# Attention on one core: the order of the maxima's products in a step, and where their results are turned and sent

## The chip, the core and the metric

One core of a Trainium2 chip: TensorE (PE, with its weight loads PEld), VectorE (DVE), ScalarE (ACT), GpSimd (POOL) and the DMA queue of SyncE (SP), each with its own queue of instructions and tied together by semaphores. The metric is the device time of one execution in microseconds, the median of the runs.

## The reference

A transformer block in float32: layer norm, attention with 32 heads of 20 columns over 2048 tokens, residual, layer norm, SwiGLU with 1728 hidden columns, residual.

```python
def _A_ref(x, wqkv, wo):            # B=1, S=2048, D=640, H=32, Dh=20
    qkv = (x @ wqkv).reshape(B, S, 3, H, Dh).transpose(2, 0, 3, 1, 4)
    q, k, v = qkv[0], qkv[1], qkv[2]
    scores = jnp.einsum("bhqd,bhkd->bhqk", q, k) * (Dh ** -0.5)
    p = _softmax(scores, axis=-1)
    o = jnp.einsum("bhqk,bhkd->bhqd", p, v)
    return o.transpose(0, 2, 1, 3).reshape(B, S, D) @ wo
def _B_ref(x, w_gate, w_up, w_down):
    return (_silu(x @ w_gate) * (x @ w_up)) @ w_down
h = x + _A_ref(_layernorm(x), A_wqkv, A_wo)
out = h + _B_ref(_layernorm(h), B_w_gate, B_w_up, B_w_down)
```

## The kernel before

The kernel has three stages: norm and projections of q, k and v; attention; output projection and feed-forward part. The change is in the attention.

Attention is cut into 32 **units**: a group `g` of four heads (8 groups) and a chunk `c` of 512 queries (4 chunks), `u = 4 g + c`. A unit has 16 **steps**, one for each tile `kt` of 128 keys. A step makes the four heads' scores (128 keys x 512 queries, L1328, functions `scores`), takes their exponential on ScalarE into `probs` (L1334), and weighs the values with the `probs` of two steps before (`weigh`, L1338, four heads at once in four column tiles of 32), summing into the bank `acc`. Heads lie in pairs in the two halves of the 128 rows: heads with `b = 0` use rows 0 to 63 of TensorE, those with `b = 1` rows 64 to 127.

The softmax subtracts each query's maximum. It must be known before a unit starts, since minus the maximum stands in extra rows of the unit's queries (`q_stk`) and is added by the score's own product. So in the steps of earlier units, **maxima** are worked out ahead: a product of 128 queries with 512 keys into one of three banks `ps_max` (L272), then a reduction on VectorE. A step makes three such banks. Two are whole ones for one head (`max_one`, reduced at L292). The third is split: the first half (256 keys, head `b = 0`) is written early in the step and the second half (256 keys, head `b = 1`) later, into the same bank, and one reduction gives both maxima (`max_half`, `max_halves`, reduced at L307). Ahead of the second half `next_half` puts a marker into TensorE's queue (L1411) that waits until the first half is written, so that the two row halves never write the bank at the same time.

The order of a step is written out by hand as a string, `ORDER`, which one loop reads letter by letter:

- `W` weighs, and runs what is due: functions put in `later` for this step, one step of the preparation of the feed-forward weights (`preparing`), and so on;
- `h` and `H`: first and second half of the split maximum; `m` and `M`: a whole one with `b = 0` and with `b = 1`;
- `S` and `s`: scores of a head with `b = 1` and with `b = 0`.

Banks of `ps_max` go round in threes, so a step's `h` takes the bank of the last step's `h`, `m` that of `m`, `M` that of `M`. The banks of the scores go round in fours.

When a unit's maxima are complete (`full`), `max_all` joins them (`neg`, L315). Then there are two ways. For units with `v % 4 == 3` and unit 1, `max_finish` turns them on TensorE (L347), ScalarE and VectorE split them into two parts (`m`), and four DMAs (L354) put them into the queries. For the others, `max_parts` splits on GpSimd, `max_turn` turns on VectorE (L331) and stores to memory, and `max_load` brings the rows back (L342).

In the second step of a unit the last weighing of the unit before is done. `row_sums` copies its `acc` to `o` on ScalarE (L1348) and sends the row sums to `r` (L1351). At later steps of that unit `reciprocals` (VectorE, L1359), `spread` (`rb`, L1367), `store_o` with a product on GpSimd (L1373) and its stores (L1376) follow. At fixed steps the loop also loads queries three units ahead (L176), and keys and values of the next group (L176, L193). All these DMAs share SP's queue, which issues in order: one that must wait holds back those behind it.

## Time and profile before

| | us |
|---|---|
| runs: median (lowest to highest of 3) | 2011.97 (2009.52 to 2014.36) |
| profiled execution, its own time | 2012.87 |
| its span | 2010.4 |
| TensorE busy, matmuls | 1985.1 (99%) |
| VectorE busy | 1599.5 (80%) |
| ScalarE busy | 1440.1 (72%) |
| GpSimd busy | 789.4 (39%) |

Busy time is the time in which at least one instruction of the engine ran. Instructions of one engine overlap, so the time from one start to the next can be shorter than the duration that the profile shows. In rows of groups the columns are line, engine, operation, output and inputs with their shapes and the count, then busy time and mean ns of one, then the engine's idle time before them and what ended it. In rows of a timeline they are start, duration, engine, line, operation, tiles, count, and in brackets the idle time before and what ended it.

### The profile page before, as it was taken

How to read it: one execution, taken by the hardware profiler on the slowest of the kernel's cores; microseconds unless marked ns; L12 is line 12 of the kernel's file. 1: busy time of each engine (PE TensorE's matmuls, PEld its weight loads, DVE VectorE, ACT ScalarE, POOL GpSimd, SP SyncE). 2: the span in 40 equal slices, each digit the busy share in tenths (PEclk: the TensorE clock that was granted, in tenths of full speed). 3: DMA queues.
4: the chain of work that ended last, by engine and by line, in shares of the span. 5: the costliest groups of instructions: out<-in, count | busy, mean ns of one | idle time of the engine just before them, and what ended most of it. 6: DMA issues, size and time to landing. Idle time of an engine off the chain costs nothing. (4 is left out here: it accounts for less than half of the span.)

```text
span 2010.4 us, 41923 instructions
## 1 busy us (share of the span) xinstructions
PE 1985.1 (99%) x14794; PEld 1268.7 (63%) x14794; DVE 1599.5 (80%) x2831; ACT 1440.1 (72%) x2827; POOL 789.4 (39%) x1182
## 2 busy tenths in 40 slices
PE   8999999999999999999999999999999999999998
PEld 6999995444444444444444444455598888888887
DVE  5687778899999899998999999975477666676667
ACT  4678778999999999999999999987633222212221
POOL 7464424343453443443400011011155544844465
PEclk9999999999999999999999999999999999999999
DMA  7887563443634544435412132222268655974642
GB/s 244 255 258 257 183 206 78 128 140 105 193 103 141 152 135 138 157 127 175 150 60 68 40 86 58 79 63 62 62 215 278 228 168 174 359 248 160 203 146 93
DMA packets 199350, 310.48 MB, mean 154 GB/s; under 512 B 53744, under 2 KB 87856, under 8 KB 198120
## 3 DMA queue, kind: packets, MB, share of 16 engines
q1 hardware_dynamic: 192552, 284.21, 44.0%
q0 software_dynamic: 6496, 23.60, 4.0%
q8 instruction: 120, 1.97, 0.4%
q14 instruction: 86, 0.70, 0.1%
q10 hardware_dynamic: 96, 0.00, 0.0%
HBM read 208.11 MB, written 99.19 MB: 153 GB/s over the span
## 5 line engine op out<-in xcount | busy, mean ns | idle before, releaser
L1334 ACT ACTIVATE probs<-ps_one 128x512 f32<-128x512 f32 x2048 | 1056.1, 612 | 46.7 <-PE ps_one L1328 37.2
L292 DVE TENSOR_REDUCE mx<-ps_max 128x1 f32<-128x512 f32 x980 | 671.8, 686 | 90.6 <-PE ps_max L272 88.0
L272 PEld LDWEIGHTS ps_max<-k_stk,q_stk 60*128 60x128 f32 x1964 | 294.2, 185 | 462.8 <-DVE mx L307 393.5
L1328 PE MATMUL ps_one<-q_stk,k_stk 62*128 62x512 f32 x2048 | 570.4, 427 | 2.7 <-DMA q_stk<-m 1.8
L272 PE MATMUL ps_max<-k_stk,q_stk 60*128 60x256 f32 (+1 forms) x1964 | 565.5, 376 | 2.5 <-DVE mx L292 1.2
L1338 PE MATMUL acc<-probs,v_stk 128*32 128x512 f32 x4096 | 546.1, 605 | 0.1
L307 DVE TENSOR_REDUCE mx<-ps_max 128x2 f32<-128x512 f32 x492 | 335.8, 683 | 0.4 <-PE ps_max L272 0.4
L1328 PEld LDWEIGHTS ps_one<-q_stk,k_stk 62*128 62x128 f32 x2048 | 304.9, 184 | 15.0 <-ACT probs L1334 11.3
L1750 DVE TENSOR_TENSOR tmp<-ps_a,tmp 128x512 f32<-128x512 f32 x208 | 141.3, 690 | 122.2 <-PE ps_a L1535 96.6
L262 DVE TENSOR_REDUCE mx<-ps_max 128x2 f32<-128x512 f32 x288 | 180.8, 685 | 63.7 <-PE ps_max L240 60.2
L252 ACT ACTIVATE ps_max<-ps_max 128x512 f32<-128x512 f32 x288 | 151.6, 583 | 42.9 <-PE ps_max L240 40.3
L1629 PE MATMUL ps_b<-halves,yp 128*128 128x320 f32 x1032 | 179.0, 308 | 1.5 <-DMA halves<-j_d 1.3
L1629 PEld LDWEIGHTS ps_b<-halves,yp 128*128 128x128 f32 x1032 | 165.2, 188 | 17.5 <-POOL yp L90 1.5
L1535 PE MATMUL ps_a<-t,units 128*128 128x512 f32 x624 | 162.5, 396 | 0.0
L1338 PEld LDWEIGHTS acc<-probs,v_stk 128*32 128x32 f32 x4096 | 80.7, 108 | 128.1 <-issue 119.9
L90 POOL TENSOR_TENSOR yp<-y,yp 128x256 fp32r<-128x256 f32 x96 | 60.2, 628 | 189.7 <-ACT yp L89 189.7
L1535 PE MATMUL ps_a<-z,units 128*128 128x512 f32 x516 | 133.8, 394 | 0.0
L1535 PEld LDWEIGHTS ps_a<-t,units 128*128 128x128 f32 x624 | 112.6, 188 | 18.5
L1373 POOL TENSOR_TENSOR o<-o,rb 128x512 f32<-128x512 f32 x31 | 39.8, 1284 | 194.2 <-DMA rb<-r_d 60.6
L1634 DVE TENSOR_TENSOR h<-ps_b,h 128x320 f32<-128x320 f32 x248 | 110.1, 482 | 6.8 <-PE ps_b L1629 5.4
L671 PE MATMUL ps_one<-z_hi,w_lo 64*128 64x512 f32 x380 | 113.4, 392 | 0.0
L671 PE MATMUL ps_one<-z_lo,w_hi 64*128 64x512 f32 x380 | 112.1, 392 | 0.0
(228 smaller groups left out, 2746.5 us busy)
## 6 DMA issues: line engine op xcount, KB each, us to landing
units<-w_d SPq DMA_DIRECT2D x186, 256.0 KB
w_d<-stage SPq DMA_DIRECT2D x106, 256.0 KB
halves<-j_d SPq DMA_DIRECT2D x70, 320.0 KB
j_d<-stage SPq DMA_DIRECT2D x42, 320.0 KB
k_stk<-k_d SPq DMA_DIRECT2D x64, 160.0 KB
q_stk<-q_d SPq DMA_DIRECT2D x64, 160.0 KB
raw<-k_d SPq DMA_DIRECT2D x62, 160.0 KB
raw<-q_d SPq DMA_DIRECT2D x54, 160.0 KB
```

Of the source, the lines that this page charges most:

```text
L252: nc.scalar.activation(ps, ps, AF.Relu)
L262: nc.vector.tensor_reduce(mx[:, b, :, t, kc], ps.rearrange("p (j n) -> p j n", j=2), axis=AX.X, op=ALU.max,)
L272: nc.tensor.matmul(ps, queries[u][rows, pair, t * P : (t + 1) * P], keys[u // NC][rows, pair, k0:k1], start=True, stop=True, skip_group_ch ...
L292: nc.vector.tensor_reduce(mx[:, b, pair, t, kc : kc + 1], ps, axis=AX.X, op=ALU.max)
L307: nc.vector.tensor_reduce(max_slots(u)[:, :, pair, t, slot], ps.rearrange("p (j n) -> p j n", j=2), axis=AX.X, op=ALU.max,)
L671: nc.tensor.matmul(ps, a[rows], b[rows], start=(i == n == 0), stop=(i == 1 and n == last), skip_group_check=True,)
L1328: nc.tensor.matmul(ps, keys[u // NC][rows, p, kt * P : (kt + 1) * P], queries[u][rows, p, :], start=True, stop=True,)
L1334: nc.scalar.activation(probs[p][:, b, :], ps, AF.Exp, scale=scale)
L1338: nc.tensor.matmul(acc[32 * j : 32 * j + 32, :], values[u // NC][:, kt, j * VW : j * VW + 32], probs[j // 2][:, j % 2, :], start=(kt == 0) ...
L1535: nc.tensor.matmul(ps.rearrange("p (t n) -> p t n", t=TPC), w[k][:, i], z[k][:, :, j], start=(first and m == 0), stop=(last and m == len(n ...
L1629: nc.tensor.matmul(ps, a, b, start=(n == 0), stop=(n == len(pairs) - 1))
L1750: add = lambda out, ps, x: nc.vector.tensor_tensor(out=out, in0=ps, in1=x, op=ALU.add)
```

## The change

```diff
-ORDER, LAST_ORDER = "WhSmsSHMs", "sSsSW"
+ORDER, LAST_ORDER = "WhSmsSMsH", "sSsSW"
...
         max_product(ps, u, t, pair, b, kc * CH, (kc + 1) * CH)
-        nc.vector.tensor_reduce(mx[:, b, pair, t, kc : kc + 1], ps, axis=AX.X, op=ALU.max)
+        return lambda: nc.vector.tensor_reduce(
+            mx[:, b, pair, t, kc : kc + 1], ps, axis=AX.X, op=ALU.max
+        )
...
         o = pc.tile([P, CH], F32, name="o", bufs=2)
-        nc.scalar.activation(o, acc, AF.Copy)
+        nc.vector.tensor_copy(o, acc)
...
             a = whole.pop(0)
-            max_one(*a)
-            counted(a[0], 1)
+            reduce = max_one(*a)
+
+            def reduced():
+                reduce()
+                counted(a[0], 1)
+
+            if b:
+                behind_half.append(reduced)
+            else:
+                reduced()
...
                     next_half(int(op == "H"))
+                    while behind_half and op == "H":
+                        behind_half.pop(0)()
...
-                    if preparing and u and kt not in (3, 4):
+                    if preparing and u and kt not in (3, 4) and not behind_step:
                         preparing.pop(0)()
...
             todo.append((u, kt, probs))
+            while behind_step:
+                behind_step.pop(0)()
             for v in full:
                 max_all(v)
                 if v % NC == NC - 1 or v == 1:
-                    later.setdefault(now[0] + 2, []).append(lambda v=v: max_finish(v))
+                    behind_step.append(lambda v=v: max_finish(v))
                 else:
                     max_parts(v)
-                    later.setdefault(now[0] + 4, []).append(lambda v=v: max_turn(v))
-                    later.setdefault(now[0] + 6, []).append(lambda v=v: max_load(v))
+                    later.setdefault(now[0] + 3, []).append(lambda v=v: max_turn(v))
+                    later.setdefault(now[0] + 5, []).append(lambda v=v: max_load(v))
...
-            if kt >= 8 and kt % 2 == 0 and c == 1 and g + 1 < NG:
+            if kt >= 8 and kt % 2 == 0 and c == (0 if g else 1) and g + 1 < NG:
                 load_keys(g + 1, slice((kt - 8) // 2 * CH, (kt - 6) // 2 * CH))
...
-            if kt == (3 if sooner else 4) and tail:
+            if kt == (3 if sooner else 5) and tail:
                 reciprocals(u - 1, tail[0][2], nc.sync)
...
-            if kt == (7 if sooner else 11) and tail:
+            if kt == (7 if sooner else 13 if c == 2 else 11) and tail:
                 store_o(u - 1, tail.pop()[1], rb, None, nc.sync)
```

The second half `H` becomes the last product of a step, behind `M` and the fourth score. The reduction of `M` is put behind that of the halves, so VectorE's order stays m, halves, M. The copy of `acc` moves from ScalarE to VectorE. `max_finish` runs at the end of the step after the one in which the maxima are complete, ahead of the next `W`, and the weights' preparation skips that step; `max_turn` and `max_load` run one step sooner. Keys are loaded in the first unit of a group, except in the first group; the reciprocals come one step later, and the stores of `o` two steps later in the third unit of a group.

TensorE's queue in one steady step, with what each waits for. Before:

```order
L1338 MATMUL acc<-probs,v_stk_5606 32x512 x4
L272 MATMUL ps_max<-k_stk_5605,q_stk 128x256 [waits DVE_49]
L1328 MATMUL ps_one<-q_stk,k_stk_5605 128x512 [waits Activation_49]
L272 MATMUL ps_max<-k_stk_5605,q_stk 128x512 [waits DVE_49]
L1328 MATMUL ps_one<-q_stk,k_stk_5605 128x512 [waits Activation_49] x2
L272 MATMUL ps_max<-k_stk_5605,q_stk 128x256 [waits PE_49,PE_sequencer_49]
L272 MATMUL ps_max<-k_stk_5605,q_stk 128x512 [waits DVE_49]
L1328 MATMUL ps_one<-q_stk,k_stk_5605 128x512 [waits Activation_49]
```

and in the change (its lines stand two further down in this part of the file):

```order
L1340 MATMUL acc<-probs,v_stk_5606 32x512 x4
L272 MATMUL ps_max<-k_stk_5605,q_stk 128x256 [waits DVE_49]
L1330 MATMUL ps_one<-q_stk,k_stk_5605 128x512 [waits Activation_49]
L272 MATMUL ps_max<-k_stk_5605,q_stk 128x512 [waits DVE_49]
L1330 MATMUL ps_one<-q_stk,k_stk_5605 128x512 [waits Activation_49] x2
L272 MATMUL ps_max<-k_stk_5605,q_stk 128x512 [waits DVE_49]
L1330 MATMUL ps_one<-q_stk,k_stk_5605 128x512 [waits Activation_49]
L272 MATMUL ps_max<-k_stk_5605,q_stk 128x256 [waits PE_49,PE_sequencer_49]
```

The whole maximum that waits for VectorE now comes where the second half stood, and the half that waits for the first half's product (PE) is last. On VectorE, the change at the second step of unit 11, where the accumulator of unit 10 is copied:

```order
L309 TENSOR_REDUCE mx_134<-ps_max 128x2
L292 TENSOR_REDUCE mx_134<-ps_max 128x1
L1350 COPY o<-acc 128x512
L292 TENSOR_REDUCE mx_134<-ps_max 128x1
L309 TENSOR_REDUCE mx_134<-ps_max 128x2
L292 TENSOR_REDUCE mx_134<-ps_max 128x1 x2
```

The copy, which stood in ScalarE's queue between two exponentials, now stands between the reduction of the last `M` and that of the next `m`. On SP's queue, the end of unit 10, where unit 11's maxima are sent (`q_stk<-m`). Before:

```order
L193 DMA v_stk_5606<-v_d 128x4x96 x2
L1376 DMA o_d<-o 20x512 x4
L1137 DMA w_d_86<-stage 128x512
L193 DMA v_stk_5606<-v_d 128x4x96
L354 DMA q_stk<-m_11431 1x8x128 x4
L1137 DMA w_d_86<-stage 128x512 x2
```

and in the change:

```order
L193 DMA v_stk_5606<-v_d 128x4x96 x2
L356 DMA q_stk<-m_11412 1x8x128 x4
L193 DMA v_stk_5606<-v_d 128x4x96
L1378 DMA o_d<-o 20x512 x4
L193 DMA v_stk_5606<-v_d 128x4x96
L1139 DMA w_d_86<-stage 128x512 x2
```

The four sends of the maxima now stand ahead of one load of values, of the stores of `o` and of a weight store.

More of the change, by code (lines that the diff above doesn't have):

```diff
@@ L1381, in tile_block @@
     left = {u: sum(2 for a in rest if a[0] == u) for u in range(1, NU)}
-    whole, halves_of = [], []
+    whole, halves_of, behind_step, behind_half = [], [], [], []
     def counted(u, n):
```

## The prediction

> **What bounds the kernel now.** I read the page's parts 1 and 5, then busy time by stretch, then one attention step on each engine, then the waits at the steps that are longer than the others. By stretch (columns: time, then busy us and instructions of PE, PEld, DVE, ACT, POOL, then granted clock, DMA share, GB/s), with the groups that the change touches:

> ```profile
> 316.00:1338.00 1022.00, 1016.77 (x7726) 435.15 (x7723) 923.72 (x1553) 1004.05 (x1964) 317.55 (x533) 1.00 0.38 114
> L307 DVE TENSOR_REDUCE mx<-ps_max 128x2 f32<-128x512 f32 x492 | 335.8, 683 | 0.4 <-PE ps_max L272 0.4
> L1348 ACT ACTIVATE o<-acc 128x512 f32<-128x512 f32 x32 | 20.1, 628 | 1.0 <-PE acc L1338 1.0
> L1650 DVE COPY own<-ps_b 128x320 f32<-128x320 f32 x32 | 14.3, 482 | 0.4 <-PE ps_b L1629 0.4
> L819 ACT ACTIVATE ev<-ps_one 128x320 f32<-128x320 f32 x32 | 14.2, 444 | 1.7 <-PE ps_one L671 1.2
> ```

> Half of the span, 1022 of 2010.4 us, is the attention with maxima: 492 steps (one L307 reduction each). TensorE, VectorE and ScalarE are all busy over 90% there, so the shares do not tell which one bounds. One steady step on TensorE does (start, duration):

> ```profile
> 703.51 0.38 PE L272 MATMUL ps_max<-k_stk,q_stk 60*128 60x256 f32 x1
> 703.51 0.50 PE L1328 MATMUL ps_one<-q_stk,k_stk 62*128 62x512 f32 x1
> 703.73 0.40 PE L272 MATMUL ps_max<-k_stk,q_stk 60*128 60x512 f32 x1
> 703.85 0.52 PE L1328 MATMUL ps_one<-q_stk,k_stk 62*128 62x512 f32 x2
> 704.08 0.34 PE L272 MATMUL ps_max<-k_stk,q_stk 60*128 60x256 f32 x1
> 704.21 0.39 PE L1328 MATMUL ps_one<-q_stk,k_stk 62*128 62x512 f32 x1
> 704.26 0.39 PE L272 MATMUL ps_max<-k_stk,q_stk 60*128 60x512 f32 x1
> 704.58 1.07 PE L1338 MATMUL acc<-probs,v_stk 128*32 128x512 f32 x8
> ```

> I call the products by the letters of the order: h and H the halves (256 columns), m and M the whole ones, s and S scores, W the weighing. From h to W it is 1.07 us. The weight loads and VectorE in the same step, with the next step's h at 705.57, so that a step is 705.57 - 703.51 = 2.06 us and W's block 0.99 of it:

> ```profile
> 704.04 0.18 PEld L272 LDWEIGHTS ps_max<-k_stk,q_stk 60*128 60x128 f32 x1
> 704.09 0.18 PEld L1328 LDWEIGHTS ps_one<-q_stk,k_stk 62*128 62x128 f32 x1
> 704.14 0.19 PEld L272 LDWEIGHTS ps_max<-k_stk,q_stk 60*128 60x128 f32 x1
> 705.57 0.18 PEld L272 LDWEIGHTS ps_max<-k_stk,q_stk 60*128 60x128 f32 x1 [0.84 <-DVE mx L307]
> 703.30 0.68 DVE L292 TENSOR_REDUCE mx<-ps_max 128x1 f32<-128x512 f32 x1
> 704.16 0.69 DVE L292 TENSOR_REDUCE mx<-ps_max 128x1 f32<-128x512 f32 x1 [0.18 <-PE ps_max L272]
> 704.77 0.68 DVE L307 TENSOR_REDUCE mx<-ps_max 128x2 f32<-128x512 f32 x1
> 705.37 0.68 DVE L292 TENSOR_REDUCE mx<-ps_max 128x1 f32<-128x512 f32 x1
> ```

> The 0.84 at 705.57 looks as if h waits for the reduction of the halves (704.77 + 0.68 = 705.45). A step in which that reduction was early says otherwise:

> ```profile
> 700.32 0.68 DVE L307 TENSOR_REDUCE mx<-ps_max 128x2 f32<-128x512 f32 x1
> 700.45 1.06 PE L1338 MATMUL acc<-probs,v_stk 128*32 128x512 f32 x8
> 701.44 0.38 PE L272 MATMUL ps_max<-k_stk,q_stk 60*128 60x256 f32 x1
> ```

> There the reduction ended at 701.00, and h still came 0.99 after W began, as in the other step. So W's block costs 0.99 whatever VectorE does, and TensorE's own chain sets the 2.06: h, S, ... H, M, W. VectorE has 0.18 of idle before m's reduction (0.26 by the spacing of 0.60 at which reductions follow each other: 703.30 + 0.60 = 703.90 to 704.16), no more.

> **The order in a step.** m keeps its place; M and s change places with H; VectorE still reduces m, halves, M. The first half's product (h) and H share a bank, so h's place depends on the same reduction as before, which keeps its time as long as H ends by 704.77. H and M use the same 64 rows of TensorE (b = 1), s the other 64. From H's weight load (704.04) to W (704.58) these two take 0.54; in the other order the columns to stream are the same 768, so W moves only if their start moves. H's load at 704.04 is set by the wait of L1411 for h to be written (h ends 703.51 + 0.38 = 703.89, then one event and its hand-over). M has no such wait; it has its own, for the bank that the previous step's M left: that reduction ends at 703.30 + 0.68 = 703.98. What an end on VectorE costs until the load, where only it is waited for:

> ```profile
> 320.82 0.69 DVE L292 TENSOR_REDUCE mx<-ps_max 128x1 f32<-128x512 f32 x1
> 321.56 0.18 PEld L272 LDWEIGHTS ps_max<-k_stk,q_stk 60*128 60x128 f32 x1 [0.50 <-DVE mx L292]
> ```

> 320.82 + 0.69 = 321.51, load at 321.56: 0.05. So M could load at 703.98 + 0.05 = 704.03, against H's 704.04 now. The wait that is removed (0.54 before W) and the wait that takes its place end within 0.01 us. The step then hangs on a loop over two steps: M's reduction, M, H, W, h, m, three reductions. From below: if M could follow S at once, the lower rows would be done early and s would be last; s began at 704.21, and with M's distance to W (704.58 - 704.26 = 0.32) W could begin at 704.53, a gain of 0.05 x 492 = 24.6 us. From above: H lies behind M and s now, and its load must come within M's stream; if it doesn't, the step grows (rival C, 0.06). I take the row that measures the wait itself: 0.00, with 0.003 for a loop without slack, +1.5 us. Queued behind M's wait are s, H and the next W; s's load (704.09) waits for ScalarE anyway, later than M's 704.03.

> [...]

> **The copy of the accumulator (L1348) goes from ScalarE to VectorE**, 31 times in the loop. On ScalarE it lengthened one step: W at

> ```profile
> 698.07 1.06 PE L1338 MATMUL acc<-probs,v_stk 128*32 128x512 f32 x8
> ```

> to 700.45 is 2.38, 0.32 over the step, and the next, 700.45 to 702.51, is 2.06. On VectorE it stands ahead of m's reduction. The trace has no such copy; bounds are the 482 ns of the 320-column copy and the 0.69 of a 512-column reduction, with a spacing of 0.60 between such instructions, which I take. 0.60 less the idle 0.26 is 0.34 that m's and all later reductions come late, and h and M after them: 0.34 against 0.32, 31 x 0.02 = +0.6 us; the loop over two steps gives half of it back, so 0. If nothing of it were covered it would be 0.60 - 0.32 = +0.28, 9 us; if M's reduction left slack, down to -0.32, -10 us.

> [...]

> **Maxima and sums sent at other times.** The waits of the long steps, by window (who <- for whom: total, times, longest), in time order; the last two are of units 2 and 10:

> ```profile
> ACT probs L1334 <- PE ps_max L272: 0.4, 1, 0.4
> ACT probs L1334 <- PE ps_max L272: 1.5, 1, 1.5
> ACT probs L1334 <- PE ps_max L272: 0.5, 1, 0.5
> ACT probs L1334 <- PE ps_max L272: 1.0, 1, 1.0
> ACT probs L1334 <- PE ps_max L272: 0.9, 1, 0.9
> PE ps_one L1328 <- DMA q_stk<-m: 1.2, 1, 1.2
> ACT probs L1334 <- PE ps_one L1328: 0.8, 3, 0.3
> DVE r L1359 <- DMA r<-o: 1.1, 1, 1.1
> ACT probs L1334 <- PE ps_one L1328: 1.2, 3, 0.8
> ```

> The first five (starts of units 10, 11, 15, 18, 19) are the first scores of a unit waiting for the rows of its maxima: 4.3 us. Why the rows are late in the 1.5 case:

> ```profile
> 687.48 0.28 DVE L90 TENSOR_TENSOR m<-ps_one,m 16x128 fp32r<-16x128 f32 x1 [0.21 <-ACT m L89]
> 687.39 1.42 SPq L1376 DMA_DIRECT2D o_d<-o  x4
> 689.93 0.35 SPq L1137 DMA_DIRECT2D w_d<-stage  x1
> 690.85 2.82 SPq L354 DMA_DIRECT2D q_stk<-m  x4
> ```

> They were ready at 687.76 and issued at 690.85, behind the stores of o and a weight store that waited for GpSimd. In the change they stand ahead of both (and of one load of values), so about 3 us sooner: enough for 1.5. The transposed kind goes one step (2.06 us) sooner, and the loads of keys that filled SP's queue ahead of it leave that unit: enough for 0.4 and 1.0. The two of 2.0 us together are VectorE waiting for r: its reciprocal goes one step later, 2.06 us against 1.1 as the wait seen. I count all 6.3 us as gone. What is late next: rb comes one step later at GpSimd, which has 4 steps to spare before it uses it (step 5 to 9) and is busy 318 of 1022 us. The 8 skipped weight steps only shift.

> **Sum.** The profiled execution took 2012.87 us (span 2010.4, 2.5 around it). 2012.87 - 6.3 + 1.5 + 0 = 2008.1. It is 0.9 above the median of the runs, 2011.97, so the forecast for the median is 2007.

> **Rivals.** (A) is this sum, own range 2003 to 2012. (B) The step shrinks as well: M is not held at 704.03, because its reduction ends sooner against it. For it: the wait of L1411 is gone and the tail is short. Against: the reductions' spacing of 0.60 is fixed and m's starts at m's end. Between 0 and 0.05 I take half: 492 x 0.025 = 12.3, 2012.87 - 6.3 - 12.3 - 0.9 = 1993. (C), slower: H's load is behind M's wait, s's load and its own event in TensorE's queue. M loads at 704.03, starts 0.11 later (as 703.73 to 703.85) and streams some 0.21, so H is to start at 704.36 and to load by 704.25. If the queue passes H only when s has started (704.21) and the event's two hand-overs of 0.05 follow, it loads at 704.31 and the step grows by 0.06: 492 x 0.06 = 29.5, so 2012.87 + 29.5 - 6.3 - 0.9 = 2035. It decides from 704.25 on; s's load at 704.09 plus the same 0.10 is 704.19, which speaks against it by little. (D) The step keeps its time and the waits stay, because the transfers themselves are slow or others take their places (keys now load in the unit before): 2012, no change.

> **The numbers.** A 0.48, B 0.20, C 0.14, D 0.18. About 0.2% (4 us) is what a measurement tells from no change: below 2008 is faster, above 2016 slower. A lies across the lower bound, 0.28 faster and 0.20 same; B is faster; C slower; D 0.12 same, 0.02 faster, 0.04 slower. Together faster 0.50, same 0.32, slower 0.18. The range takes in half of B and all of A and D: 1993 to 2018.

> **What would show it.** A: steady steps of 2.06 to 2.07 us, with M's load 0.05 behind an L292 reduction's end; the q_stk<-m waits and r's wait at or near nothing; a step of about 2.4 at each unit's start still, now behind a VectorE copy. B: steps of 2.01 to 2.05. C: steps over 2.10 and H's load 0.27 or more behind M's. D: the five waits still there. The forecast is wrong if the steady step moves by more than 0.01 us in either direction, since 492 steps multiply it.

## The result, and the profile after

| us | before | changed |
|---|---|---|
| median (lowest to highest of 10 runs each) | 2012.38 (2009.52 to 2014.36) | 2023.85 (2014.56 to 2041.16) |
| profiled execution, its own time | 2012.87 | 2039.48 |
| its span | 2010.4 | 2037.7 |

The ratio is 1.0071, 95% interval 1.0049 to 1.0094: slower, where 2007 was forecast and 2018 was the upper end of the range. The changed kernel's runs also lie 27 us apart, those of before 5. Its profiled execution is the second longest of its ten, so it shows more loss than the median has.

First the steady step of the changed kernel, the one that the prediction is about: the weight loads of W, h, M and H in two steps (those of the other products left out), then VectorE's reductions that M waits for (start, duration, then the instruction; the line numbers are two higher here).

```profile
708.36 0.16 PEld L1340 LDWEIGHTS acc<-probs,v_stk 128*32 128x32 f32 x8 [0.20 <-issue]
709.35 0.18 PEld L272 LDWEIGHTS ps_max<-k_stk,q_stk 60*128 60x128 f32 x1 [0.84 <-DVE mx L309]
709.83 0.18 PEld L272 LDWEIGHTS ps_max<-k_stk,q_stk 60*128 60x128 f32 x1
709.99 0.18 PEld L272 LDWEIGHTS ps_max<-k_stk,q_stk 60*128 60x128 f32 x1
710.37 0.16 PEld L1340 LDWEIGHTS acc<-probs,v_stk 128*32 128x32 f32 x8 [0.19 <-issue]
711.36 0.18 PEld L272 LDWEIGHTS ps_max<-k_stk,q_stk 60*128 60x128 f32 x1 [0.84 <-DVE mx L309]
711.95 0.18 PEld L272 LDWEIGHTS ps_max<-k_stk,q_stk 60*128 60x128 f32 x1 [0.17 <-DVE mx L292]
712.11 0.18 PEld L272 LDWEIGHTS ps_max<-k_stk,q_stk 60*128 60x128 f32 x1
712.49 0.16 PEld L1340 LDWEIGHTS acc<-probs,v_stk 128*32 128x32 f32 x8 [0.20 <-issue]
...
709.09 0.68 DVE L292 TENSOR_REDUCE mx<-ps_max 128x1 f32<-128x512 f32 x1
711.21 0.68 DVE L292 TENSOR_REDUCE mx<-ps_max 128x1 f32<-128x512 f32 x1
```

W follows W after 710.37 - 708.36 = 2.01 and then after 2.12; the steps alternate so, and their mean is the 2.07 of before. M's load waits for the reduction of its bank: it ends at 709.09 + 0.68 = 709.77, M loads at 709.83, and in the next step 711.89 and 711.95. H's load follows M's by 0.16. The step is what the prediction's sum says.

The time is lost elsewhere. The row of the weighing products (busy, mean ns, then idle time ahead of them) of the kernel before, then the same row of the changed kernel, with its row of the scores, its instruction queue q8 (packets, MB, share) and the count of each engine's instructions:

```profile
L1338 PE MATMUL acc<-probs,v_stk 128*32 128x512 f32 x4096 | 546.1, 605 | 0.1
```

```profile
L1340 PE MATMUL acc<-probs,v_stk 128*32 128x512 f32 x4096 | 556.1, 608 | 8.9 <-issue 8.8
L1330 PE MATMUL ps_one<-q_stk,k_stk 62*128 62x512 f32 x2048 | 571.2, 429 | 7.2 <-issue 5.4
q8 instruction: 120, 1.97, 0.4%
PE 1994.4 (98%) x14794; PEld 1282.5 (63%) x14794; DVE 1620.2 (80%) x2863; ACT 1422.6 (70%) x2795; POOL 792.7 (39%) x1182
```

"issue" is idle time for which the profile names no releaser: nothing that TensorE waits for is late, and it stands still. By the waits of one stretch of 16 us of the changed kernel (who <- for whom: total, times, longest):

```profile
DVE mx L292 <- PE ps_max L272: 9.2, 3, 7.8
ACT probs L1336 <- PE ps_one L1330: 8.8, 2, 7.5
PEld acc L1340 <- issue: 7.4, 5, 6.3
PE acc L1340 <- issue: 5.4, 1, 5.4
```

VectorE and ScalarE wait for TensorE there, and TensorE for nothing. On its timeline the stop lies in the middle of a W block, six products of eight done:

```profile
752.14 1.06 PE L1340 MATMUL acc<-probs,v_stk 128*32 128x512 f32 x6
758.63 1.87 PE L1340 MATMUL acc<-probs,v_stk 128*32 128x512 f32 x2 [5.43 <-issue]
762.21 1.93 PE L1340 MATMUL acc<-probs,v_stk 128*32 128x512 f32 x8
```

```profile
DMA  4650920000067920000007400100199226467999
q1 hardware_dynamic: 2269, 2.80, 41.3%
q14 instruction: 1, 0.01, 0.1%
```

```profile
q1 hardware_dynamic: 436, 0.30, 105.9%
q8 instruction: 1, 0.02, 5.3%
```

For 23 us no block came on q8, though the DMA engines stood idle in several parts of that time (the zeros), and 2.5 us after TensorE had stopped one did. Counted in the trace's order, TensorE stopped at the same place of a block of 256 here and at each of the ten stops of over 0.3 us that the attention's steady part of this execution has, 19.4 us together: its count since the span's start is each time 193 above a multiple of 256, so the blocks end there. Over all kernels of this study 53 stops lie at a block's end, in eight of them. All 53 end 1.2 to 1.9 us after the packet of the next block has landed (its start and its duration added); 50 of them end 2.2 to 3.0 us after its start, and the packets of the other three took 2.5 to 3.5 us. The other stops of over 0.3 us there, behind the attention's first step, are waits for maxima, their rows or their bank, 0.3 to 1.2 us each: four in the kernel before, four in order_alone, and eight of 0.3 in hold_each. The profile calls most of the 53 "issue"; the rest it puts down to an instruction that had ended long before, as here:

```profile
1103.60 0.68 DVE L292 TENSOR_REDUCE mx<-ps_max 128x1 f32<-128x512 f32 x1
1106.08 0.39 PE L272 MATMUL ps_max<-k_stk,q_stk 60*128 60x512 f32 x1 [1.37 <-DVE mx L292]
```

That reduction ended at 1104.28.

A stop can cost more than itself, as the granted clock shows (stretch, then busy us and instructions by engine, then clock, DMA share, GB/s):

```profile
753.00:758.60 5.60, 0.20 (x3) 0.00 (x0) 0.66 (x2) 0.72 (x2) 1.26 (x1) 0.91 0.93 225
758.60:764.00 5.40, 5.37 (x18) 1.68 (x17) 1.98 (x3) 2.17 (x4) 3.19 (x6) 0.50 0.66 196
908.40:910.40 2.00, 0.03 (x1) 0.00 (x0) 0.00 (x0) 0.60 (x2) 0.00 (x0) 1.00 0.40 124
911.20:914.50 3.30, 3.30 (x18) 1.52 (x16) 1.88 (x4) 2.01 (x4) 0.00 (x0) 0.50 0.97 331
```

With two stops of 5.4 us and one of 2.06 the granted clock fell to half, for 6.8, 6.8 and 3.4 us. Of these, 1.1 us of the first and 3.4 of the second still lay within the stop (1174.00 to 1177.40: clock 0.50, matmuls 0.02 us busy), so TensorE ran some 12.5 us at half clock: 6.3 us more. The W block at 762.21 takes 1.93 instead of 1.06.

How late a block is asked for can be read from the trace: number the packets and the blocks, and count how many instructions TensorE has begun in its block when the packet of the next one starts (0: at once; 256: when nothing is left). The request itself leaves no record; the start of its packet stands for it. The DMA engines do not keep it waiting: in the changed kernel 52 of 62 packets start over 5 us after TensorE has begun the block, and in 43 of these 52 cases there was a stretch of over 0.3 us in between in which no other packet was under way (3.9 us in all, on average over the 52). Worked out so for one profiled execution of each kernel, in the 60 to 63 blocks of the attention's steady part:

```
kernel           median us   late: mean, largest   over 200   stops at a block's end
before             2012.38     41   123                0        0
changed            2023.85    158   256               21       10, 19.4 us
order_undone       2006.70     44   112                0        0
sends_alone        2006.53     49   146                0        0
order_alone        2027.35    154   256               16        7,  9.4 us
keys_undone        2029.21    151   256               17        9, 15.9 us
copy_undone        2013.69    139   245                8        3,  3.4 us
reduce_at_once     2024.03    151   256               17        8, 10.3 us
m_before_h         2029.97    161   256               23       10, 15.8 us
marker_early       2009.02    114   207                1        0
marker_idle        2022.69    105   207                1        0
marker_quarter     2012.86    132   256               11        3,  5.2 us
hold_two           2018.92    139   256                7        2,  3.2 us
hold_each          2080.04     89   167                0        0
h_s_m              2005.75     92   158                0        0
```

(m_before_h has one more stop, of 2.17 us, at the end of the block behind these. The expectations below speak of 124 and 234 for the changed kernel: there a request that came only after its block had run dry was counted from the new block.)

### The profile page after: what moved, and what is told of

It reads as the page before. It is cut to its first block, busy times and chain, and to the rows that moved or that the text cites. A ratio compares the mean times of both kernels' runs of the same rounds, so it can differ in the third digit from the quotient of the medians.

```text
span 2037.7 us, 41837 instructions
## 1 busy us (share of the span) xinstructions
PE 1994.4 (98%) x14794; PEld 1282.5 (63%) x14794; DVE 1620.2 (80%) x2863; ACT 1422.6 (70%) x2795; POOL 792.7 (39%) x1182
## 5 line engine op out<-in xcount | busy, mean ns | idle before, releaser
L292 DVE TENSOR_REDUCE mx<-ps_max 128x1 f32<-128x512 f32 x980 | 670.6, 684 | 94.8 <-PE ps_max L272 79.5
L272 PEld LDWEIGHTS ps_max<-k_stk,q_stk 60*128 60x128 f32 x1964 | 315.7, 185 | 474.5 <-DVE mx L309 370.9
L272 PE MATMUL ps_max<-k_stk,q_stk 60*128 60x256 f32 (+1 forms) x1964 | 570.3, 377 | 5.9 <-issue 2.4
L1340 PE MATMUL acc<-probs,v_stk 128*32 128x512 f32 x4096 | 556.1, 608 | 8.9 <-issue 8.8
L90 POOL TENSOR_TENSOR yp<-y,yp 128x256 fp32r<-128x256 f32 x96 | 60.5, 630 | 189.5 <-ACT yp L89 189.5
```

The source lines that it names most:

```text
L272: nc.tensor.matmul(ps, queries[u][rows, pair, t * P : (t + 1) * P], keys[u // NC][rows, pair, k0:k1], start=True, stop=True, skip_group_ch ...
L292: return lambda: nc.vector.tensor_reduce(mx[:, b, pair, t, kc : kc + 1], ps, axis=AX.X, op=ALU.max)
L1340: nc.tensor.matmul(acc[32 * j : 32 * j + 32, :], values[u // NC][:, kt, j * VW : j * VW + 32], probs[j // 2][:, j % 2, :], start=(kt == 0) ...
```

## Experiments

**1. Which part does it.** Undone alone, of the changed kernel: the order, the earlier keys, the copy; and the order alone in the kernel before.

order_undone (changed kernel):

```
-ORDER, LAST_ORDER = "WhSmsSMsH", "sSsSW"
+ORDER, LAST_ORDER = "WhSmsSHMs", "sSsSW"
...
-            if b:
-                behind_half.append(reduced)
-            else:
-                reduced()
+            reduced()
```

> The change with the old order of a step (H before M, M reduced at once), all its other edits kept. If the new order makes TensorE run out of instructions (theory order): no idle time of TensorE put down to 'issue' over 0.5 us, steady steps of 2.06 to 2.07 us, and 2004 to 2009 us, since the waits for maxima and row sums (6.3 us) stay away. If the keys' earlier loads do it (theory keys): TensorE still stops for 1 to 6 us at some of the first units of a group, and 2015 to 2030 us.

order_alone (kernel before):

```
-ORDER, LAST_ORDER = "WhSmsSHMs", "sSsSW"
+ORDER, LAST_ORDER = "WhSmsSMsH", "sSsSW"
...
-            max_one(*a)
-            counted(a[0], 1)
+            reduce = max_one(*a)
...
+            if b:
+                behind_half.append(reduced)
+            else:
+                reduced()
...
+                    while behind_half and op == "H":
+                        behind_half.pop(0)()
```

> The kernel before with the new order of a step alone. Theory order: stops of TensorE with nothing to wait for (1 to 6 us each) appear though the keys load where they did, 2020 to 2035 us. Theory keys: none; the step's mean stays at 2.065 us, 2011 to 2014 us.

keys_undone (changed kernel):

```
-            if kt >= 8 and kt % 2 == 0 and c == (0 if g else 1) and g + 1 < NG:
+            if kt >= 8 and kt % 2 == 0 and c == 1 and g + 1 < NG:
```

> The change with the keys loaded in the second unit of each group again, all else kept. Theory keys: the stops go, 2006 to 2010 us. Theory order: they stay, in other units, 2015 to 2035 us.

copy_undone (changed kernel):

```
-        nc.vector.tensor_copy(o, acc)
+        nc.scalar.activation(o, acc, AF.Copy)
```

> The change with the accumulator's copy on ScalarE again. Both theories: the stops stay and the time is that of the change within its own spread, 2015 to 2035 us; the second and third step of a unit take 0.3 us more than two steady ones in either case. If VectorE's copy were the cause: below 2010 us.

Measured against the kernel before on the same chip (2014.27): order_undone 2006.70, ratio 0.9966 (0.9954 to 0.9978); order_alone 2027.35, 1.0067 (1.0046 to 1.0089); keys_undone 2029.21, 1.0076 (1.0057 to 1.0095); copy_undone 2013.69, 1.0000 (0.9991 to 1.0010). The order alone makes a loss as large as the whole change has, and without it the rest of the change is faster than before. The weighing row of order_undone, then of order_alone, shows both:

```profile
L1340 PE MATMUL acc<-probs,v_stk 128*32 128x512 f32 x4096 | 545.3, 605 | 0.0
```

```profile
L1340 PE MATMUL acc<-probs,v_stk 128*32 128x512 f32 x4096 | 553.1, 607 | 7.9 <-issue 7.9
```

Undoing the keys takes nothing of it away. copy_undone missed its expectation: its blocks are asked for late as well (mean 139), but fewer of them over 200 instructions late (8, not 21), and it stops three times for 3.4 us (its profiled execution is the shortest of its ten, so the stops are fewer there than at the median; the times of its runs, 2011.37 to 2017.42, are shorter all the same). Why the copy's engine moves the tail of that distribution stays open; with the old order it makes no difference (below).

**2. Which part of the order.** The marker ahead of H (L1421) was a suspect: the author's theory was that in the old order it holds TensorE's instruction reader, since H's load comes only 0.15 us behind h's end (704.04 and 703.89 in the prediction's step); in the new one it stands behind M, and h has long ended. Three kernels, and one for the terms of the sum.

marker_early (changed kernel), a marker ahead of M too:

```
                 if op in "mM":
+                    if op == "M" and halves_of and halves_of[0][2]:
+                        nc.tensor.keepalive_nop([nc.tensor.lower_ap(halves_of[0][2][0])])
```

> The changed kernel with one more marker of the split maximum's bank, ahead of the last whole product M instead of only behind it; the products' order, the deferred reduction, the copy and the sends as in the changed kernel. Theory marker: TensorE's instruction reader asks for the next 256 instructions while its sequencer is held, and in the new order the marker stands behind M, where the first half h has long ended, so nothing holds it. With a marker that waits ahead of M again, the requests come on average 30 to 70 instructions behind a block's start (changed kernel 124, kernel before 41), no stop of TensorE over 1 us is left, and the time is 2005 to 2012. Theory place: the order of the products alone makes the requests late; they stay over 100 instructions late, stops of 8 us or more in all remain, and the time is 2014 to 2040.

reduce_at_once (changed kernel), with VectorE's old order:

```
-            if b:
-                behind_half.append(reduced)
-            else:
-                reduced()
+            reduced()
```

> The changed kernel with the new order of products, but VectorE reduces the last whole product M where it is issued, ahead of the split one's halves. Theory VectorE: the deferred reduction holds TensorE so that its requests come late; undone, they come under 70 instructions behind a block's start and the time is 2005 to 2012. Theories marker and place: TensorE's own order is what counts, the requests stay over 100 instructions late, stops of 8 us or more in all remain, and the time is 2014 to 2045 (the halves now wait for one more reduction of 0.4 us, which may lengthen the step as well).

m_before_h (changed kernel):

```
-ORDER, LAST_ORDER = "WhSmsSMsH", "sSsSW"
+ORDER, LAST_ORDER = "WhSmsSMHs", "sSsSW"
```

> The changed kernel with a third order: the last whole product M, then the second half H, then the step's last score (W h S m s S M H s). Theory marker: the marker still stands behind M, so the requests stay over 100 instructions late and stops remain, 2014 to 2045. Theory place, if it is H as a step's last product that matters: the requests come under 70 instructions late, no stop over 1 us, 2005 to 2015.

sends_alone (order_undone):

```
-        nc.vector.tensor_copy(o, acc)
+        nc.scalar.activation(o, acc, AF.Copy)
```

> The kernel with the old order and the sends of the change, and with the copy of the finished sums on ScalarE again: of the change only the maxima and sums that are turned and sent at other times are left. By the prediction's terms the sends carry 6.3 us and the copy nothing: 2006 to 2009, beside 2006.7 for the same kernel with the copy on VectorE. Rival: the copy carries half or more of the gain, then 2010 to 2013.

Against 2012.58: marker_early 2009.02, ratio 0.9982 (0.9971 to 0.9992); reduce_at_once 2024.03, 1.0061 (1.0041 to 1.0080); m_before_h 2029.97, 1.0096 (1.0065 to 1.0127); sends_alone 2006.53, 0.9968 (0.9957 to 0.9979). (The 0.4 us that the expectation of reduce_at_once gives for one more reduction is too little by the rows, where reductions follow each other at 0.60.) VectorE's order is not the cause, and neither is H as the last product: with M ahead of H and a score behind it the stops are there (15.8 us). sends_alone equals order_undone within the intervals: with the old order the sends carry the gain and the copy nothing. marker_early hit on time and stops and missed on its reason: the blocks were still asked for 114 instructions late, where 30 to 70 were expected; only the tail was cut, to 207. So the wait at the marker is not what lets a request out, or not alone.

**3. The marker's wait, or one more instruction.** marker_idle has as many instructions a step as marker_early, but the second marker beside the first, where nothing waits; marker_quarter has the early marker in every fourth step. marker_idle (changed kernel):

```
-            nc.tensor.keepalive_nop([nc.tensor.lower_ap(banks[0])])
+            for _ in range(2):
+                nc.tensor.keepalive_nop([nc.tensor.lower_ap(banks[0])])
```

> The changed kernel with a second marker beside the first, both behind the last whole product M, so that TensorE gets as many instructions a step as in the kernel with a marker ahead of M (2009.0 us), but none that waits ahead of M. Theory marker: it is the wait ahead of M that lets the requests for instructions through, so here stops of 8 us or more in all remain and the time is 2014 to 2045. Theory count: one more instruction a step, waiting or not, shifts or eases the requests; then no stop over 1 us and 2005 to 2012.

marker_quarter (changed kernel):

```
+                    if op == "M" and kt % 4 == 2 and halves_of and halves_of[0][2]:
+                        nc.tensor.keepalive_nop([nc.tensor.lower_ap(halves_of[0][2][0])])
```

> The changed kernel with the additional marker ahead of M in every fourth step only. Theory marker: a request that is due goes out in a step with such a marker, so more than half of the requests in the steady steps 3 to 15 of a unit fall into the quarter of steps that have one (or the step behind it), none is over about 200 instructions late, and the time is 2005 to 2014. If the requests are spread over the steps as in the changed kernel, a marker's wait does not release them, and stops and 2014 to 2040 are to be expected.

Against 2013.34: marker_idle 2022.69, ratio 1.0057 (1.0038 to 1.0076); marker_quarter 2012.86, 0.9998 (0.9988 to 1.0008). marker_idle falls between the two theories: as slow as theory marker said, and without a single stop in its profiled execution. Its time goes into the step, which alternates 2.02 and 2.19: by the medians of the 16 steps a unit takes 33.94 against 33.42 in the changed kernel, and 30 x 0.52 = 16 us is the difference to order_undone. So the stops were gone with a marker that waits for nothing (none in marker_idle) as with one that waits (none in marker_early). In marker_quarter a due request went out in 13 of 54 steps with an early marker and in 24 of the 137 others from step 3 on: no difference that would carry theory marker, though the time lies in its range. The theory falls.

**4. Holding the reader longer.** A marker behind H, meant to keep W's loads back until H has ended: in steps 4 and 8 of a unit (hold_two), or in all from 3 on (hold_each). hold_two (changed kernel); in hold_each the condition is `now[0] % NT >= 3`:

```
             max_half(banks[0], i, *a, b)
+            if now[0] % NT in (4, 8):
+                nc.tensor.keepalive_nop([nc.tensor.lower_ap(banks[0])])
```

> The changed kernel with a marker behind the second half H in steps 4 and 8 of each unit, which holds TensorE's next weighing block until H has ended (an estimated 0.15 to 0.3 us a held step, some 58 held steps: 9 to 17 us). Theory hold: a due request goes out in a step in which TensorE's instruction reader stands held for long; then in those steps, where the changed kernel sends hardly any due request (2 to 5 of 100), more than half of the due ones go out, no stop over 1 us is left, and the time is 2015 to 2026. Theory place: the requests stay as rare in steps 3 to 8, stops stay, and the holds come on top: 2030 to 2055.

> The same hold in every step from 3 to 15 of a unit, some 385 of them: the time grows by 55 to 110 us to 2065 to 2120, which is not the question. Theory hold: the requests come 20 to 60 instructions behind a block's start on average, none over 130 (changed kernel 124 and 234), and TensorE has no stop over 1 us. Theory place: they stay over 90 late on average.

Against 2012.08: hold_two 2018.92, ratio 1.0024 (1.0014 to 1.0035), its held steps 2.33 instead of 2.11; hold_each 2080.04, 1.0335 (1.0319 to 1.0350), all steps 2.25. In the held steps of hold_two a due request went out 3 times in 25, and stops remained, 2.6 and 0.5 us: theory hold falls too, though the time lies in its range. Holding every step brings the mean to 89 and the largest to 167, without a stop; that is neither theory's forecast.

**5. M ahead of H's marker, or a maximum as the last product.** In h_s_m the order is W h S m s S H s M (from order_undone).

```
-ORDER, LAST_ORDER = "WhSmsSHMs", "sSsSW"
+ORDER, LAST_ORDER = "WhSmsSHsM", "sSsSW"
```

> A fourth order, W h S m s S H s M, with the last whole product reduced where it is issued; copy and sends as in the change. H and its marker stand ahead of M as in the old order, but M comes last, behind the score. Theory ahead: what makes the requests late is M, which waits for VectorE, ahead of H's marker; here it stands behind it, so the requests come 30 to 70 instructions late, no stop over 1 us, 2005 to 2012. Theory last: a maximum product as a step's last makes them late, whichever it is; then over 100 late with stops, 2014 to 2040.

Against 2013.83: 2005.75, ratio 0.9961 (0.9947 to 0.9975). Its profiled execution was one at a granted clock of 0.95 from first to last (2018.18 us, the longest of its ten), so only its counts are read: no stop at a block's end, requests at most 158 late. Time and stops are those of theory ahead, and theory last falls; the mean of 92 is again more than the 30 to 70 expected. It is the fastest kernel of the study, though not told apart from order_undone and sends_alone.

**What stays open.** Why requests go out rarely when M stands ahead of H. Pooled over the kernels with the old order (before, order_undone, sends_alone) and those of experiments 1 and 2 with M ahead of H and one marker (the changed kernel, order_alone, keys_undone, copy_undone, reduce_at_once, m_before_h), so many of the steps in which a request was due at the step's start saw it go out:

```
step of the unit    M behind H    M ahead of H
0                   13 of 20       39 of 122
1, 2                21 of 22      103 of 150
3 to 8              34 of 69       34 of 465
9 to 15             64 of 111     167 of 820
```

With the old order every second step takes its chance; with the new one, one in fourteen in steps 3 to 8 and one in five behind them. In the first steps of a unit, which are longer and uneven, both orders send. No cause beyond that was found: not a marker's wait, not a longer hold. Taking the marker out of the old order was not tried, since it is there to keep h and H from writing one bank at the same time.

## Why the prediction was wrong

**The order.** The step itself came out as the sum says, and its reasons held: M's load waits for its own bank's reduction and comes 0.06 behind it, H's load comes 0.16 behind M's and not the 0.27 of rival C (its start 0.24 behind M's at 709.93 and 0.34 behind M's at 711.95, where C took some 0.21 for M to stream), and a unit of 16 steps takes 33.42 us by the medians of its steps, against 33.43 before. The step was also called a loop over two steps, which is how it runs, 2.01 and 2.12. H, the shorter last product, lets W follow 0.21 behind its start (708.15 and 708.36), where W came 0.32 behind M's; but H starts later than M did, and the step gains nothing. (Of the 492 reductions that the prediction counts in the stretch of 1022 us, 480 lie in it.) So rivals B and C were wrong in mechanism; C's 2035 resembles the result by accident, since no step grew.

The step that failed is the first, "TensorE's own chain sets the 2.06", as far as the sum takes it for all that TensorE needs: 492 steps times a step's time, plus the waits that the profile names. TensorE also needs its instructions, 256 at a time, and the order of the products changes how late they are asked for (41 instructions on average before, 154 in order_alone). The sum had no term for that; in the changed kernel's profiled execution it was ten stops of 19.4 us together. The page of before had one row on it, 120 packets with a 0.4% share, which looks like nothing. Nothing else in that profile shows a shortage, because none had happened: the latest request came at 123 of 256. The prediction also said that it is wrong if the steady step moves by more than 0.01 us. It did not move, and the forecast was wrong all the same.

The amount: the changed kernel's profiled span is 2037.7 - 2002.6 = 35.1 us over that of order_undone, of which 19.4 are stops and 6.3 the half clock behind them. Of the other 9.4, a later start of the attention is 1.1, 3.4 us at half clock just behind it, which order_undone does not have, 1.7, and the parts behind the steady stretch 1.8; the rest stays open. Between the medians it is 17 us. That the stops differ from run to run, and so make the spread of 27 us, is likely but seen in one execution alone: the mean granted clock, known for every run, goes from 0.998 in the fastest to 0.994 in the two slowest.

In the kernel before, none of the 61 block ends cost a stop; in the changed kernel ten cost 19.4 us. Half clock came with its stops of 5.43, 5.41 and 2.06 us, the last by the rows of 908 to 914 above, and not with those of 1.67, 1.41 and 1.37. The length alone does not decide: in order_alone half clock followed a stop of 1.52 us and not one of 2.23.

**The copy.** Right in the step: 0.34 was to replace 0.32 a unit, "so 0". By the medians of its 16 steps a unit takes 33.42 with the copy on VectorE (order_undone) and 33.44 with it on ScalarE (sends_alone), and the two kernels differ by less than their intervals. What was expected as one step of 2.4 is spread over three (2.08, 2.12, 2.22). In the change itself the term was not 0: with the new order the copy's engine is worth 10 us (2013.69 with it on ScalarE, 2023.85 on VectorE), and that goes with the stops and not with the step.

**The sends.** Right, in kind and size: 6.3 us were counted, and sends_alone is 6.05 below the kernel before. The waits of the whole attention in before (the starts of units, q_stk and r), then in order_undone:

```profile
ACT probs L1334 <- PE ps_max L272: 4.5, 5, 1.5
DVE r L1359 <- DMA r<-o: 2.6, 2, 1.6
PE ps_one L1328 <- DMA q_stk<-m: 1.8, 2, 1.2
```

```profile
DVE r L1361 <- DMA r<-o: 0.4, 1, 0.4
PE ps_max L272 <- DVE mx L292: 0.2, 1, 0.2
```

The rows for ScalarE at a unit's start and for q_stk are gone, and r's wait is 0.4. Rival D is out.

So the sum without the order's hidden price was good: it forecast a gain of 4.8, or 6.3 without its 1.5 for the order, and with the old order 7.6 was measured on one chip (order_undone) and 6.05 on another (sends_alone). That 2006.70 stands so close to the 2007 forecast is in part luck, since the kernel before took 2014.27 there. The price itself was in no rival.

## What to carry to other kernels

When an engine stops and the profile names nothing it waits for, count its instructions: here 53 stops lay at a block's end of 256, and all ended 1.2 to 1.9 us after a 16 KB packet on the instruction queue had landed, so instructions were missing and not data. Before changing the order on an engine that is busy from end to end, read in the old trace how late its blocks are asked for. The margin here is, by an estimate, the distance to some 215 and not to 256: from the packet's start to the first instruction of its block it took 2.2 to 3.0 us in 50 of the 53 stops, and in 2.5 us TensorE begins some 40 instructions (33.4 in 2.07 us). The steady step, 33.42 us a unit against 33.43, said nothing of it. Measure parts of a change apart: here one part was worth -6 us and another +17, and the change alone shows only their sum.

## What was not expected of the hardware

The packet of the next block of instructions did not start at once when a block began: in the kernel before TensorE had begun 41 of the block's 256 instructions on average, in the changed one 158, and in order_alone, which has the instructions of before in the same number and only their order differs, 154. TensorE did not stop where the packet came soon enough: over all kernels no stop over 0.3 us followed a packet that started at up to 224 instructions, but for three packets (207, 217, 219) that took 2.5 to 3.5 us themselves; at 228 the changed kernel stopped for 0.37 and 0.42 us, and the stopping kernels all reach 245 or more. One more instruction a step, even one that waits for nothing, took the stops away (none in marker_idle, one execution), and by lengthening the step (33.94 us a unit against 33.42) cost about as much as they had (2022.69 against 2023.85).
